# LN2 tiles 2 and 3 turned by VectorE and a DRAM round trip in a DiT block

## The chip, the cores and the metric

The kernel runs on one core of a Trainium2 chip. The metric is device time in microseconds for one execution. Three runs of the kernel before took 243.12, 242.97 and 244.42 us; their median is 243.12 us.

The engines in this document are TensorE (PE; its weight loads are shown apart as PEld), VectorE (DVE), ScalarE (ACT), GpSimd (POOL) and SyncE (SP), which here only issues DMAs. Data lies in SBUF (128 partitions), matmul results in PSUM (8 banks), weights and scratch tensors in DRAM.

## The reference: one diffusion-transformer block

Batch 2, 256 tokens each (512 tokens together), D = 1152, 2 heads of 576, MLP width 4608, everything in bf16:

```python
mod = (_silu(c) @ w_mod).reshape(B, 6, 1, D)
shift_a, scale_a, gate_a, shift_m, scale_m, gate_m = [mod[:, i] for i in range(6)]
h = _layernorm(x) * (1 + scale_a) + shift_a
q, k, v = split(h @ wqkv)                       # per head
a = softmax(q k^T * Dh**-0.5) v @ wo
x = x + gate_a * a
h2 = _layernorm(x) * (1 + scale_m) + shift_m
m = _gelu(h2 @ w_fc1) @ w_fc2
return x + gate_m * m
```

## The kernel before

**Tiling.** Tokens are cut in four tiles of 128 (tile t, batch b = t // 2), D in KT = 9 blocks of 128, the MLP width in JT = 36 blocks of 128. A matmul contracts over the 128 partitions, so before fc1 the normalised tokens must be turned: from `XN2[t]` (token on the partition, 1152 features along it) to the fc1 operand `H2T` (feature on the partition, tokens along it).

**Who orders the work.** The code records every operation with what it reads and writes. TensorE and SyncE keep the order in which the code states them; the other engines' orders come from a list scheduler with modelled costs that always takes the ready operation with the longest modelled way to the end. Waits are then put in from the recorded reads and writes. So a DMA that SyncE issues is never overtaken by one that stands later in the code, and SyncE stops at the first DMA whose wait is not over.

**The stretch around the change.**

- `wo_tile(t)` multiplies by wo in three chunks of 384 columns. Per chunk VectorE multiplies by the gate (L1165), GpSimd adds x (L1166), VectorE takes the LayerNorm statistics (L740). After the third come L741, L743, the `pow` on GpSimd (L744) and L1170 on VectorE, and ScalarE writes the normalised tile `XN2[t]` (L1171).
- `xn2_T(t)` turns a tile: nine 128x128 TensorE transposes (L695) into PSUM, then nine evacuations that apply scale and shift, on VectorE (L1187) and ScalarE (L1190).
- `fc1_tile(f, tok0, ntok)` is one unit of nine matmuls (L692) into one of four rotating PSUM banks; ScalarE reads the bank with a Gelu (L1200) into `GT[f]`. The first F0 = 9 blocks are done in halves: first for tokens 0 to 255, which need only tiles 0 and 1, and later for tokens 256 to 511. Blocks 9 to 35 are done for 512 tokens at once. The transposes of tile 2 stand after the fourth first half, those of tile 3 after the seventh.
- fc1's weights come in nine loads of four blocks each (`wfc1_load(q)`, 1152 KB) into four buffers. Load q = 4, for blocks 16 to 19, goes into the buffer of blocks 0 to 3, and may start once block 3's second half is done; it must have landed before block 16 starts.
- fc2's weights come in four loads of 2592 KB (`ld_wfc2_0` to `_3`). `ld_wfc2_1` and `_2` are issued before the attention output, `ld_wfc2_3` after the fc1 first halves, since its space holds `XN2` too. `ld_wfc2_0` is the last, since its space holds the mlp gate's weights.
- `mlp_gate` computes gate_m on VectorE: 18 operations over 1152 columns (L1092, L1095), a transpose and a reduction (L1099, L1101), and small steps, ordered after the last `h2T` evacuation. The gate goes through DRAM (`dit_scratch`) and is first read when fc2 starts.

SyncE's order from the middle of the kernel on is thus: fc1 loads 0 and 1, the two attention gates, fc1 loads 2 and 3, the mlp gate's weights (`ld_gm`, 2592 KB), `ld_wfc2_1`, `_2`, `_3`, fc1 loads 4 to 8, `ld_wfc2_0`, and the output stores. All its DMAs are recorded at line L673.

Of the kernel before, what the change touches and what calls it, by code (L numbers as in the profile page):

```python
# [73 lines left out]
TRACK_DRAM = set()  # L74
# [417 lines left out]
BF16 = mybir.dt.bfloat16  # L492
F32 = mybir.dt.float32
ALU = mybir.AluOpType
# [3 lines left out]
P = 128  # L498
NTOK = 512
D = 1152  # L500
KT = 9
# [4 lines left out]
SCALE = DH ** -0.5  # L506
CH = 384
NCH = 3
F0 = 9
KC = 5  # L510
KG = 6
NG = 9
# [3 lines left out]
def c_mm(n):  # L516
    return max(n / 2.4 + 2.5, 27.0)


def c_act(n, aps=0):  # L520
    return 190.0 + 0.8 * n + 75.0 * aps
# [18 lines left out]
def c_dve_32(n):  # L540
    return 110.0 + 1.15 * n


def build_kernel(nc, x, c, wqkv, wo, w_mod, w_fc1, w_fc2, out):
# [2 lines left out]
    scratch_t = nc.dram_tensor("dit_scratch", (2, 2, KT * P), BF16)  # L547
    TRACK_DRAM.add("dit_scratch")
    scratch = scratch_t.ap()
    with (  # L550
        nc.sbuf_tensor("arena", [P, ARENA_BYTES // 2], BF16) as arena,
        nc.psum_tensor("psum", [P, 4096], F32) as psum,
# [2 lines left out]
        def sb(off, nbytes, dt=BF16):  # L555
            assert off % 4 == 0 and off + nbytes <= ARENA_BYTES, (off, nbytes)
            v = arena[:, off // 2:(off + nbytes) // 2]
            if dt == F32:
                v = v.bitcast(F32)
            return v  # L560

        def ps32(bank, c0=0, n=512):
            return psum[:, bank * 512 + c0: bank * 512 + c0 + n]

        def ps16(bank, c0=0, n=1024):
            v = psum[:, bank * 512: (bank + 1) * 512].bitcast(BF16)
            return v[:, c0:c0 + n]
# [7 lines left out]
        O_HK = O_HX + 9216  # L575
# [7 lines left out]
        def misc(nbytes):  # L583
            o = mo[0]
            mo[0] += (nbytes + 3) // 4 * 4
            assert mo[0] <= ARENA_BYTES
            return o

        def wmat(o, f):
            return sb(o, KT * f * 2).rearrange("p (k f) -> p k f", k=KT)  # L590
# [12 lines left out]
        WFC2 = sb(O_R, 4 * W1).rearrange("p (k f) -> p k f", k=JT)  # L603
        WFC1 = [wmat(o, 512) for o in (O_A, O_A + 9216, O_C, O_C + 9216)]
# [3 lines left out]
        HK = sb(O_HK, 9216).rearrange("p (k t) -> p k t", k=KT)  # L608
# [1 line left out]
        Q4B = sb(O_Q4B, 1024)  # L610
        X1 = sb(O_QK, 18432, F32).rearrange("p (t d) -> p t d", t=4)
        V = sb(O_HK, 9216).rearrange("p (t d) -> p t d", t=4)
        H2T = HK
        OT = sb(O_HX, 9216).rearrange("p (k t) -> p k t", k=KT)
        PP = [sb(O_P + i * 1024, 1024).rearrange("p (j k) -> p j k", j=2) for i in range(4)]
        PTS = [sb(O_PT + i * 1024, 1024).rearrange("p (j k) -> p j k", j=2) for i in range(4)]
# [2 lines left out]
        XN2 = [sb(O_R + 4 * W1 - (i + 1) * 2304, 2304) for i in range(4)]  # L619
# [25 lines left out]
        SHM = MT[:, 0:288]  # L645
        SC1M = sb(misc(72), 72, F32)
# [22 lines left out]
        wfc2_v = w_fc2.rearrange("(k p) f -> p k f", p=P)  # L669

        def dma(dst, src, nbytes, name, is_out=False, eng="sp", run=4096):
            eff = 1.0 if run >= 4096 else (1.08 if run >= 2304 else (1.15 if run >= 1536 else (1.3 if run >= 1024 else 1.42)))
            return S.op(eng, 500.0 if eng == "sp" else 150.0, lambda e: e.dma_start(dst, src), reads=[src], writes=[dst],  # L673
                        name=name, dma_bytes=nbytes * eff, is_out=is_out)

        def dve(cost, fn, reads, writes, name):
            return S.op("dve", cost, fn, reads=reads, writes=writes, name=name)

        def act(cost, fn, reads, writes, name):
            return S.op("act", cost, fn, reads=reads, writes=writes, name=name)  # L680
# [10 lines left out]
        def mm(o, l, r, st, sp, **kw):  # L691
            S.instr(lambda e: e.matmul(o, lhsT=l, rhs=r, start=st, stop=sp, **kw), reads=[l, r], writes=[o])  # L692

        def tr(o, i_, idn):
            S.instr(lambda e: e.transpose(o, i_, idn), reads=[i_, idn], writes=[o])  # L695
# [59 lines left out]
        for t in range(4):  # L755
# [13 lines left out]
            for part, c0, c1 in ((("a", 0, KC * P), ("b", KC * P, D)) if t == 3 else (("", 0, D),)):  # L769
                xi, xo = X[:, t, c0:c1], XN[:, t, c0:c1]  # L770
                dve(c_dve_fast(c1 - c0), lambda e, xi=xi, xo=xo, m=m, rs=rs: e.tensor_scalar(out=xo, in0=xi, scalar1=m, scalar2=rs,
                                                                                           op0=ALU.subtract, op1=ALU.mult),
# [184 lines left out]
        for kt in range(KT):  # L957
            for b in range(2):
                src, dst = HK[:, kt, b * 256:(b + 1) * 256], HX[:, kt, b * 256:(b + 1) * 256]
                s2 = SHA[:, kt * 32 + b:kt * 32 + b + 1]  # L960
# [159 lines left out]
        def pv_halves():  # L1120
            S.unit("pe", 4 * c_mm(256) + 100.0, "PV_halves")
            for b in range(2):
                for kjt in range(2):
                    for h in range(2):
                        f0 = 512 + 64 * h
                        mm(psum[64 * h:64 * h + 64, 5 * 512 + b * 256:5 * 512 + b * 256 + 256], V[:, 2 * b + kjt, f0:f0 + 64],
                           PTS[b * 2 + h][:, kjt, :], b == 0 and kjt == 0, b == 1 and kjt == 1, skip_group_check=True,
                           tile_position=(0, 64 * h))
            S.order_after(copy_on("dve", OT[:, 4, :], ps32(5), 512, False, "OT_ev_4"), last_mt[0])
# [18 lines left out]
        def acc_bank():  # L1148
            b = acc[acc_rr[0] % len(acc)]
            acc_rr[0] += 1  # L1150
            return b
# [21 lines left out]
        last_h2T = [None]  # L1173

        def xn2_T(t):
            b = t // 2
            xn2 = XN2[t]
            S.unit("pe", KT * c_mm(128), "xn2T_%d" % t)
            hi, lo = ((7, 6), (1, 0))[t % 2]
            slot = [ps16(hi, kt * 128, 128) if kt < 4 else ps16(lo, (kt - 4) * 128, 128) for kt in range(KT)]  # L1180
            for kt in range(KT):
                tr(slot[kt], xn2[:, kt * 128:(kt + 1) * 128], IDENT)
            for kt in range(KT):
                o, dst = slot[kt], H2T[:, kt, t * 128:(t + 1) * 128]
                s1, s2 = SC1M[:, kt * 2 + b:kt * 2 + b + 1], SHM[:, kt * 32 + b:kt * 32 + b + 1]
                if kt < (4 if t < 2 else 6):
                    last_h2T[0] = dve(335, lambda e, o=o, dst=dst, s1=s1, s2=s2: e.tensor_scalar(out=dst, in0=o, scalar1=s1, scalar2=s2, op0=ALU.mult, op1=ALU.add),  # L1187
                        [o, s1, s2], [dst], "h2T_%d_%d" % (t, kt))
                else:
                    act(440, lambda e, o=o, dst=dst, s1=s1, s2=s2: e.activation(out=dst, in_=o, func=ACTF.Identity, scale=s1, bias=s2),  # L1190
                        [o, s1, s2], [dst], "h2T_%d_%d" % (t, kt))

        def fc1_tile(f, tok0, ntok):
            q = f // 4
            S.unit("pe", KT * c_mm(ntok), "fc1_%d_%d" % (f, tok0))
            o = ps32(acc_bank(), 0, ntok)
            for kt in range(KT):
                mm(o, WFC1[q % 4][:, kt, (f % 4) * 128:(f % 4) * 128 + 128], H2T[:, kt, tok0:tok0 + ntok], kt == 0, kt == KT - 1)
            dst = GT[f][:, tok0:tok0 + ntok]
            act(c_act(ntok), lambda e: e.activation(out=dst, in_=o, func=ACTF.Gelu_apprx_tanh), [o], [dst], "gelu_%d_%d" % (f, tok0))  # L1200

# [38 lines left out]
        wfc1_load(2)  # L1240
        wfc1_load(3)
        dma(WGM, wmod_v[:, :, 5 * D:6 * D], D * D * 2, "ld_gm", run=2304)
        for q4 in range(1, 3):
            dma(WFC2[:, 9 * q4:9 * q4 + 9, :], wfc2_v[:, 9 * q4:9 * q4 + 9, :], 9 * P * D * 2, "ld_wfc2_%d" % q4, run=2304)
        pv_halves()
        for b in range(2):
            for h in range(2):
# [2 lines left out]
        wo_tile(1)  # L1250
        wo_tile(2)
        xn2_T(0)
        wo_tile(3, {2: lambda: xn2_T(1)})
        for f in range(0, 4):
            fc1_tile(f, 0, 256)
        xn2_T(2)
        for f in range(4, F0 - 2):
            fc1_tile(f, 0, 256)
        xn2_T(3)
        for f in range(F0 - 2, F0):  # L1260
            fc1_tile(f, 0, 256)
        dma(WFC2[:, 27:36, :], wfc2_v[:, 27:36, :], 9 * P * D * 2, "ld_wfc2_3", run=2304)
        mlp_gate(last_h2T[0])
        k = acc_rr[0] % 4
        acc[:] = [6, 7] + acc[k:] + acc[:k]
        acc_rr[0] = 0
        for f in range(F0):
            fc1_tile(f, 256, 256)
        for f in range(F0, JT):
            if f % 4 == 0 and f // 4 >= 4:  # L1270
# [6 lines left out]
        for t in range(4):  # L1277
            b = t // 2
# [3 lines left out]
            for (c0, c1) in pieces:  # L1282
                w = c1 - c0
                S.unit("pe", JT * c_mm(w), "fc2_%d_%d" % (t, c0))
                o = ps32(acc_bank(), 0, w)
# [22 lines left out]
def bass_standalone__dit_block__diffusion_kernel(  # L1308
    nc: bass.Bass,
    x: bass.AP,  # L1310
    c: bass.AP,
    wqkv: bass.AP,
    wo: bass.AP,
    w_mod: bass.AP,
    w_fc1: bass.AP,
    w_fc2: bass.AP,
    out: bass.AP,
):
    build_kernel(nc, x, c, wqkv, wo, w_mod, w_fc1, w_fc2, out)
# [28 lines left out]
```

## Time and profile before

| What | us |
|---|---|
| Median of the runs (lowest, highest) | 243.12 (242.97, 244.42) |
| Span of the profiled execution | 242.5 |
| TensorE busy, with 1699 matmuls | 237.3 (98%) |
| VectorE busy | 121.5 (50%) |
| ScalarE busy | 67.8 (28%) |
| GpSimd busy | 19.9 (8%) |

The span runs from the first to the last instruction. The profiled execution has no other time of its own than this span; it lies 0.6 us under the median and 0.5 us under the fastest run, which also hold what lies around the span.

In the rows of the profile, L673 is a line of kernel.py; out<-in names what is written and read; nearly every SBUF tensor is a part of one array and so is called `arena`. PE is matmul time, PEld weight loads that run beside it.

### The profile page before, as it was taken

Reading aid. Unit: us, or ns where it says so; the run is one execution under the profiler, and the core shown is the slowest. Engines: PE = TensorE matmul, PEld = TensorE weight load, DVE = VectorE, ACT = ScalarE, POOL = GpSimd, SP = SyncE. Lnnn points to the kernel's source line nnn. Section 1 sums busy time; section 2 is a strip of 40 time slices with the busy share of each in tenths; the row PEclk is TensorE's granted clock in tenths of the full one; section 3 lists DMA queues with packets and bytes.
Section 4 is the critical chain, followed back from the end, with each engine's and each line's share of the span. In section 5 each row is a group of like instructions: output and inputs, shape, how many; then the busy total and the mean of one; then the engine's idle time right before and its main releaser. Section 6 shows DMA issues by size and latency. Waiting matters only on the chain.

```text
span 242.5 us, 3957 instructions
## 1 busy us (share of the span) xinstructions
PE 237.3 (98%) x1699; PEld 145.4 (60%) x1699; DVE 121.5 (50%) x229; ACT 67.8 (28%) x136; POOL 19.9 (8%) x36
## 2 busy tenths in 40 slices
PE   6899999999999999999999999999999999999995
PEld 2688844466666666898544444444666566566564
DVE  2654379988996689669999700000022222111112
ACT  4921440435524206973233322222000000000000
POOL 1300000000002276400000110000000000000000
PEclk9979999999999999999999999999999999999999
DMA  6999999999992999999963499100000000000000
GB/s 221 378 370 392 389 392 390 398 413 402 391 352 79 312 374 391 391 348 398 352 198 83 157 313 374 43 0 3 0 16 19 16 16 16 19 16 16 21 27 20
DMA packets 30363, 51.58 MB, mean 213 GB/s; under 512 B 1547, under 2 KB 15755, under 8 KB 30347
## 3 DMA queue, kind: packets, MB, share of 16 engines
q1 hardware_dynamic: 29888, 50.73, 58.9%
q0 software_dynamic: 288, 0.60, 0.8%
q8 instruction: 13, 0.21, 0.4%
q10 hardware_dynamic: 171, 0.01, 0.0%
q14 instruction: 3, 0.02, 0.0%
HBM read 50.15 MB, written 1.19 MB: 212 GB/s over the span
## 4 chain that ended last, share of the span: by engine, by line
PE 95%; DMA 3%; SPq 1%; DVE 0%; issue 0%
PE psum L692 93%; DMA arena<-in_wqkv_dram 3%; PE psum L695 2%; SPq L673 1%; DVE arena L1290 0%; DVE arena L1291 0%
## 5 line engine op out<-in xcount | busy, mean ns | idle before, releaser
L692 PE MATMUL psum<-arena 128*128 128x384 bf16 (+8 forms) x1610 | 234.0, 314 | 2.4 <-POOL arena L718 1.5
L692 PEld LDWEIGHTS psum<-arena 128*128 128x128 bf16 (+2 forms) x1610 | 139.7, 97 | 92.4 <-issue 3.8
L1290 DVE TENSOR_TENSOR arena<-psum,arena 128x384 f32<-128x384 f32 (+2 forms) x13 | 6.8, 526 | 88.6 <-PE psum L692 88.6
L1200 ACT ACTIVATE arena<-psum 128x512 bf16<-128x512 f32 (+1 forms) x45 | 22.8, 512 | 42.1 <-PE psum L692 42.1
L687 ACT ACTIVATE arena<-psum 128x512 bf16<-128x512 f32 (+6 forms) x34 | 18.2, 560 | 37.9 <-PE psum L692 37.9
L1064 DVE SCALAR_TENSOR_TENSOR arena<-arena 128x1152 f32<-128x1152 bf16 x16 | 21.9, 1408 | 0.0
L1095 DVE SCALAR_TENSOR_TENSOR arena<-arena 128x1152 f32<-128x1152 bf16 x16 | 21.4, 1414 | 0.0
L1166 POOL TENSOR_TENSOR arena<-arena 128x384 f32<-128x384 f32 x12 | 10.9, 912 | 11.7 <-DVE arena L1165 9.5
L740 DVE BATCH_NORM_STATS2 arena<-arena 128x6 f32<-128x384 f32 (+1 forms) x18 | 9.5, 549 | 3.8 <-DMA arena<-in_x_dram 3.8
L673 POOL DMA_DIRECT2D dit_scratch<-arena x4 | 2.4, 609 | 96.6 <-DVE arena L1082 60.3
L689 DVE CAST arena<-psum 128x512 bf16<-128x512 f32 x11 | 7.2, 687 | 5.3 <-PE psum L692 5.3
L1165 DVE TENSOR_TENSOR arena<-psum,arena 128x384 f32<-128x384 f32 x12 | 6.7, 556 | 3.7 <-PE psum L692 3.7
L1171 ACT ACTIVATE arena<-arena 128x1152 bf16<-128x1152 f32 x4 | 5.4, 1344 | 9.8 <-DVE arena L1170 9.8
L695 PE MATMUL psum<-arena 128*128 128x128 bf16 (+1 forms) x89 | 7.4, 225 | 0.4 <-DMA arena<-in_c_dram 0.4
L695 PEld LDWEIGHTS psum<-arena 128*128 128x128 bf16 (+1 forms) x89 | 6.3, 102 | 2.2 <-DMA arena<-in_c_dram 1.1
L1291 DVE TENSOR_TENSOR arena<-arena 128x384 bf16<-128x384 f32 (+2 forms) x13 | 6.9, 527 | 0.5
L1190 ACT ACTIVATE arena<-psum,arena 128x128 bf16<-128x128 bf16 x16 | 6.1, 455 | 3.0 <-PE psum L695 2.2
L1187 DVE TENSOR_SCALAR arena<-psum,arena 128x128 bf16<-128x128 bf16 x20 | 5.5, 336 | 2.9 <-PE psum L695 2.9
L1009 ACT ACTIVATE arena<-psum,arena 128x256 bf16<-128x256 f32 x8 | 3.7, 471 | 0.2 <-DVE arena L1006 0.2
L744 POOL TENSOR_TENSOR arena<-arena 128x1 f32<-128x1 f32 x6 | 3.3, 555 | 4.7 <-DVE arena L743 4.5
L1005 DVE TENSOR_REDUCE arena<-psum 128x2 f32<-128x512 f32 x4 | 2.8, 688 | 0.9 <-PE psum L692 0.7
L962 ACT ACTIVATE arena<-arena 128x256 bf16<-128x256 bf16 x6 | 2.5, 495 | 1.5 <-DVE arena L956 1.5
(60 smaller groups left out, 53.9 us busy)
## 6 DMA issues: line engine op xcount, KB each, us to landing
arena<-in_w_fc_dram SPq DMA_DIRECT2D x9, 1152.0 KB, 8.0
arena<-in_w_fc_dram SPq DMA_DIRECT2D x4, 2592.0 KB, 17.6
arena<-in_wqkv_dram SPq DMA_DIRECT2D x18, 288.0 KB, 9.3
arena<-in_w_mod_dram SPq DMA_DIRECT2D x6, 864.0 KB, 12.3
arena<-in_w_mod_dram SPq DMA_DIRECT2D x3, 1728.0 KB, 20.5
arena<-in_wqkv_dram SPq DMA_DIRECT2D x1, 2592.0 KB, 17.6
arena<-in_wo_dram SPq DMA_DIRECT2D x1, 2592.0 KB, 24.9
arena<-in_w_mod_dram SPq DMA_DIRECT2D x1, 2592.0 KB, 18.5
```

Of the source, the lines that this page charges most:

```text
L687: act(c_act(n), lambda e: e.activation(out=dst, in_=src, func=ACTF.Copy), [src], [dst], name)
L689: return dve(c_dve_psum16(n) if psum16 else c_dve_psum32(n), lambda e: e.tensor_copy(dst, src), [src], [dst], name)
L692: S.instr(lambda e: e.matmul(o, lhsT=l, rhs=r, start=st, stop=sp, **kw), reads=[l, r], writes=[o])
L695: S.instr(lambda e: e.transpose(o, i_, idn), reads=[i_, idn], writes=[o])
L740: dve(550, lambda e, s=s, o=o: e.bn_stats(out=o, in_=s), [s], [o], "bn_%s_%d" % (tag, ci))
L1064: ga_units[(b, kt)] = dve(150 + FG * 1.1, lambda e, o=o, w=w, s1=s1: e.scalar_tensor_tensor(out=o, in0=w, scalar=s1, in1=o, op0=ALU.mult, ...
L1095: u = dve(1300, lambda e, o=o, w=w, s1=s1: e.scalar_tensor_tensor(out=o, in0=w, scalar=s1, in1=o, op0=ALU.mult, op1=ALU.add), [w, s1, o], ...
L1165: dve(550, lambda e, o=o, ga=ga, x1c=x1c: e.tensor_tensor(out=x1c, in0=o, in1=ga, op=ALU.mult), [o, ga], [x1c], "wo_t1_%d_%d" % (t, ci))
L1166: S.op("pool", 930, lambda e, xs=xs, x1c=x1c: e.tensor_tensor(out=x1c, in0=x1c, in1=xs, op=ALU.add), reads=[x1c, xs], writes=[x1c], name=" ...
L1200: act(c_act(ntok), lambda e: e.activation(out=dst, in_=o, func=ACTF.Gelu_apprx_tanh), [o], [dst], "gelu_%d_%d" % (f, tok0))
L1290: dve(c_dve_psum32(w), lambda e, o=o, gm=gm, t1=t1: e.tensor_tensor(out=t1, in0=o, in1=gm, op=ALU.mult), [o, gm], [t1], "fc2_t1_%d_%d" % ( ...
L1291: dve(c_dve_32(w), lambda e, t1=t1, x1c=x1c, ost=ost: e.tensor_tensor(out=ost, in0=t1, in1=x1c, op=ALU.add), [t1, x1c], [ost], "fc2_out_%d ...
```

## The change

Tiles 0 and 1 are turned as before; tiles 2 and 3 no longer by TensorE.

- `xn2_turn(t)`: one VectorE instruction transposes all 32x32 blocks of `XN2[t]` (36 blocks for each group of 32 tokens), reading the features with a step of four, and SyncE stores the result to a DRAM tensor `h_turn[t]`, 288 KB, one run of 2304 bytes per partition.
- `xn2_back(t)`: SyncE loads the tile back, four runs of 576 bytes per partition, which puts each feature on its partition; nine VectorE operations apply scale and shift in place.
- The fc1 operand `H2T` lies in the same bytes in another order: 16 groups of 32 tokens, and in each group the nine feature blocks. A matmul over 256 or 512 tokens now reads runs of 32 tokens (64 bytes), 576 bytes apart, for all four tiles.
- F0 goes from 9 to 14: five more fc1 blocks are done in halves, and no transposes stand among them.
- `ld_wfc2_1` and `_2` are stated after the fc1 first halves, right before `ld_wfc2_3`. In SyncE's order the two stores and two loads of the turn stand where they stood.
- All nine evacuations of tiles 2 and 3 are on VectorE; of tiles 0 and 1, four are on VectorE and five on ScalarE as before.

```diff
-F0 = 9
+F0 = 14
@@ build_kernel
+    p_turn = nc.dram_tensor("p_turn", (4, P, 512), BF16).ap()
+    h_turn = nc.dram_tensor("h_turn", (4, P, D), BF16).ap()
...
-        H2T = HK
+        H2T = sb(O_HK, 9216).rearrange("p (g k i) -> p k g i", g=16, k=KT)
+        H2F = [sb(O_HK + t * 2304, 2304) for t in range(4)]
@@ xn2_T
-                o, dst = slot[kt], H2T[:, kt, t * 128:(t + 1) * 128]
+                o, dst = slot[kt].rearrange("p (g i) -> p g i", i=32), H2T[:, kt, 4 * t:4 * t + 4, :]
...
-                if kt < (4 if t < 2 else 6):
+                if kt < 4:
...
+        def xn2_turn(t):
+            src, flat = XN2[t].rearrange("p (k x c) -> p c k x", k=KT, c=4), H2F[t]
+            dve(c_dve_32(D), lambda e: e.transpose(flat, src), [src], [flat], "h2turn_%d" % t)
+            dma(h_turn[t], flat, P * D * 2, "st_h2_%d" % t)
+
+        def xn2_back(t):
+            b, flat = t // 2, H2F[t]
+            dma(flat.rearrange("p (a y) -> p a y", a=4), h_turn[t].rearrange("(a x) (c y) -> (x c) a y", a=4, c=4), P * D * 2, "ld_h2_%d" % t)
+            for kt in range(KT):
+                dst = H2T[:, kt, 4 * t:4 * t + 4, :]
+                s1, s2 = SC1M[:, kt * 2 + b:kt * 2 + b + 1], SHM[:, kt * 32 + b:kt * 32 + b + 1]
+                last_h2T[0] = dve(200, lambda e, dst=dst, s1=s1, s2=s2: e.tensor_scalar(out=dst, in0=dst, scalar1=s1, scalar2=s2, op0=ALU.mult, op1=ALU.add),
+                    [dst, s1, s2], [dst], "h2T_%d_%d" % (t, kt))
@@ fc1_tile
-                mm(o, WFC1[q % 4][:, kt, (f % 4) * 128:(f % 4) * 128 + 128], H2T[:, kt, tok0:tok0 + ntok], kt == 0, kt == KT - 1)
+                mm(o, WFC1[q % 4][:, kt, (f % 4) * 128:(f % 4) * 128 + 128], H2T[:, kt, tok0 // 32:(tok0 + ntok) // 32, :], kt == 0, kt == KT - 1)
@@ main sequence
         dma(WGM, wmod_v[:, :, 5 * D:6 * D], D * D * 2, "ld_gm", run=2304)
-        for q4 in range(1, 3):
-            dma(WFC2[:, 9 * q4:9 * q4 + 9, :], wfc2_v[:, 9 * q4:9 * q4 + 9, :], 9 * P * D * 2, "ld_wfc2_%d" % q4, run=2304)
         pv_halves()
...
         wo_tile(3, {2: lambda: xn2_T(1)})
-        for f in range(0, 4):
+        xn2_turn(2)
+        xn2_turn(3)
+        xn2_back(2)
+        xn2_back(3)
+        for f in range(0, F0):
             fc1_tile(f, 0, 256)
-        xn2_T(2)
-        for f in range(4, F0 - 2):
-            fc1_tile(f, 0, 256)
-        xn2_T(3)
-        for f in range(F0 - 2, F0):
-            fc1_tile(f, 0, 256)
+        for q4 in range(1, 3):
+            dma(WFC2[:, 9 * q4:9 * q4 + 9, :], wfc2_v[:, 9 * q4:9 * q4 + 9, :], 9 * P * D * 2, "ld_wfc2_%d" % q4, run=2304)
         dma(WFC2[:, 27:36, :], wfc2_v[:, 27:36, :], 9 * P * D * 2, "ld_wfc2_3", run=2304)
         mlp_gate(last_h2T[0])
```

(`p_turn` is not used by any instruction.)

More of the change, by code (lines that the diff above doesn't have):

```diff
@@ L549, in build_kernel @@
     scratch = scratch_t.ap()
+    p_turn = nc.dram_tensor("p_turn", (4, P, 512), BF16).ap()
+    h_turn = nc.dram_tensor("h_turn", (4, P, D), BF16).ap()
+    TRACK_DRAM.add("p_turn")
+    TRACK_DRAM.add("h_turn")
     with (
```

## The prediction

> **What bounds the kernel now.** I read the chain of work that ended last, then the timeline around the change, then when each weight load lands. The chain, in order of time (start, length):
>
> ```profile
> 93.25 0.50 PE psum L695 x9
> 93.75 2.92 PE psum L692 x18
> 96.68 0.50 PE psum L695 x9
> 97.18 5.39 PE psum L692 x45
> 102.57 0.50 PE psum L695 x9
> 103.08 2.95 PE psum L692 x27
> 106.02 0.50 PE psum L695 x9
> 106.53 133.56 PE psum L692 x810
> ```
>
> TensorE never waits here: the end moves by what is added to or taken from its queue. The four groups of nine at L695 are the transposes of LN2, 0.50 us each. 27 matmuls of 256 columns take 2.95, so a half tile of fc1 takes 0.983 and fc1 starts at 102.57 - 4 x 0.983 = 98.64. The Gelus of the full tiles follow each other by 1.942 (timeline):
>
> ```profile
> 130.96 0.37 SPq L673 DMA_DIRECT2D arena<-in_w_fc_dram  x1
> 130.97 0.60 ACT L1200 ACTIVATE arena<-psum 128x512 bf16<-128x512 f32 x1 [1.35 <-PE psum L692]
> 132.91 0.60 ACT L1200 ACTIVATE arena<-psum 128x512 bf16<-128x512 f32 x1 [1.34 <-PE psum L692]
> ```
>
> The DMA at 130.96 is fc1 load 7, which waits for block 15; so block 16 starts at 130.9 (by sum 98.64 + 18 x 0.983 + 1.0 + 7 x 1.942 = 130.9). That is the point I compare.
>
> The second thing is SyncE's queue. Issue to landing, for `ld_gm` with `ld_wfc2_1`, then `ld_wfc2_2`, `ld_wfc2_3`, fc1 loads 4 and 6, each from a stretch that holds its issue:
>
> ```profile
> arena<-in_w_mod_dram SPq DMA_DIRECT2D x1, 2592.0 KB, 18.5
> arena<-in_w_fc_dram SPq DMA_DIRECT2D x1, 2592.0 KB, 21.0
> ...
> arena<-in_w_fc_dram SPq DMA_DIRECT2D x1, 2592.0 KB, 24.3
> ...
> arena<-in_w_fc_dram SPq DMA_DIRECT2D x1, 2592.0 KB, 11.2
> ...
> arena<-in_w_fc_dram SPq DMA_DIRECT2D x1, 1152.0 KB, 8.6
> ...
> arena<-in_w_fc_dram SPq DMA_DIRECT2D x1, 1152.0 KB, 5.5
> ```
>
> With their issues at 79.0, 83.3, 86.6, 106.6, 112.45 and 123.2 the first five land at 97.5, 104.3, 110.9, 117.8 and 121.05: in the order of issue, one 2592 KB load every 6.8 us (390 GB/s), an 1152 KB load 3.2 after the one ahead. Load 6 went out on an empty queue and took 5.5, so 2.3 is fixed. Load 4 lands 9.9 us before block 16 needs it.
>
> **The change, part by part.**
>
> *Transposes of tiles 2 and 3 go:* -2 x 0.50 = -1.0 on the path. *Five more blocks in halves:* 5 x (2 x 0.983 - 1.942) = +0.1.
>
> *Operand in runs of 32 tokens.* The nearest rows are the 72 matmuls of 2x288 for the modulation rows, whose moving operand is read in runs of 32 columns, 256 bytes apart, four at a time in four strips of the array (busy time by stretch; us, PE, PEld, DVE, ACT, POOL, clock, DMA share, GB/s):
>
> ```profile
> 68.90:71.20 2.30, 2.30 (x74) 1.65 (x72) 2.30 (x3) 0.49 (x1) 0.00 (x0) 1.00 1.10 348
> ```
>
> 18 groups of 288 columns in 2.2 to 2.3 us are 122 to 128 ns a group, the pace of contiguous operands (384 columns in 162 ns: 122 for 288). So I take 0. If 64-byte runs at a pitch of 576 cost a tenth, that is 0.1 a half tile and 0.19 a full one.
>
> *Statistics.* The scheduler now puts tile 2's aggregation behind two of tile 3's statistics. In the trace these run from 99.2 by 0.54 each; so tile 2's variance is ready at 101.1 rather than 99.3, `pow` (0.55) ends at 101.75, and ScalarE writes XN2 2 from 102.0 (101.0 before) and XN2 3 from 103.3 to 104.6 (1.34 each). The Gelu of block 2 stands behind both, and block 6 needs its bank at 104.4: it starts near 105.0, so +0.6. Block 16's weightless start is then 130.9 - 1.0 + 0.1 + 0.6 = 130.6.
>
> *The turn.* Transposes of 1152 f32 took 1356 ns, of 2304 2578 (1.06 a column); 96 bf16 took 267 against 278 for 96 f32, so bf16 is no faster there. Two by 1.36: 103.4 to 104.75 and to 106.0. Stores: an output store of 96 KB lands in 1.6, one of 20 KB in 1.4, so 288 KB in about 2.1: 106.9 and 108.2. Loads of 288 KB: 2.3 + 0.8 by load 6; a scratch load of that size took 4.3, the slowest 6.6; with runs of only 576 bytes I take 3.4. SyncE issues load 2 at 106.95 and load 3, which waits for store 3, at 108.3; they land at 110.4 and 111.7. Eighteen evacuations at 0.15 to 0.2 (twelve of 256 columns at L965 are 2.4 us busy) end at 113.2. TensorE comes to the second halves at 98.64 + 14 x 0.983 + 0.6 = 113.0 and to the ninth feature block at 113.9. It doesn't wait, with under a microsecond to spare; the five extra half tiles are that cover.
>
> *What is queued behind the turn.* All three fc2 loads now stand behind load 3 of the turn on SyncE, and fc1 load 4 behind them. So:
> - `ld_wfc2_1` is issued at 108.3 + 0.4 = 108.7 (83.3 before) and lands at 108.7 + 2.3 + 6.8 = 117.8, `_2` at 124.6, `_3` at 131.4;
> - fc1 load 4 (its buffer is free at 113.0 + 3.9 = 116.9) lands 3.2 later, at 134.6.
>
> Block 16 is ready at 130.6, so TensorE waits 4.0 us there. This wait swallows what came before it: the gained 0.9 and the 0.6. Block 16 starts at 134.6 instead of 130.9: **+3.7**. Nothing later is late: load 5 lands at 137.8 and is needed at 142.4; load 8 waits for block 19 as before; `mlp_gate` starts 5 us later (113.2 for 108.1) and its gate lands near 155, `ld_wfc2_0` near 157, fc2 starts near 173.5 (130.9 + 20 x 1.942 + 3.7).
>
> Sum: 242.5 + 3.7 = 246.2 for the profiled span; the median lies 0.6 above the span, so **246.8**.
>
> Bounds of the landing. Low: turn 3 costs 0.6, stores 1.6, and 9.14 MB move at 415 GB/s (the best stretches): issue at 107.3, landing at 131.6, +0.7. High: stores take 4.3 like the scratch rows, the loads run at 360 GB/s as from 84 to 88 us: issue at 110.8, landing at 138.5, +7.6. I stand near the middle, as four landings in a row went by 6.6 to 6.9.
>
> The Trainium skill, "DMA: Bandwidth & Descriptors", Specifications, gives a fabric ceiling of 435 GB/s and an HBM limit of about 358 per core; by the first load 4 would land at an estimated 132.0 (+1.1), by the second at 136.5 (+5.6). The landings here, 390, lie between.
>
> **Rivals.**
>
> *The clock falls in the wait.* The trace shows it once, early, after a stretch of short matmuls with gaps (clock is the third number from the right):
>
> ```profile
> 10.00:12.00 2.00, 1.79 (x25) 1.43 (x26) 1.69 (x8) 1.97 (x3) 0.46 (x1) 0.79 1.04 408
> 12.00:14.00 2.00, 2.00 (x11) 1.44 (x10) 1.68 (x4) 0.79 (x2) 0.00 (x0) 0.50 1.05 387
> 14.00:16.00 2.00, 2.00 (x22) 1.88 (x21) 0.96 (x4) 0.00 (x0) 0.55 (x1) 0.86 1.13 356
> ```
>
> What is missing from 1.00 adds up to 2 x (0.21 + 0.50 + 0.14) = 1.7 us, some 3.4 us at half clock. If 4.0 us of idleness set this off, +1.7: 248.5. Against it: no wait of such length occurs in the trace. The Trainium skill, "TensorE: Matmul & The Clock Gate", Part 1, says that one free-running window of about 3.4 us without work halves the clock; by that rule a wait of 4.0 holds a whole window about one time in six, and partly idle windows decide the rest.
>
> *Not slower: the loads come in time.* If load 4 landed by 130.6, the time would be 242.8 (-1.0 + 0.1 + 0.6), or 242.2 without the Gelu's delay. That needs 9.14 MB in 19.6 us, 466 GB/s, which no stretch shows, or `ld_wfc2_1` issued at 104.7, before the second transpose can end. In part it can be: within 1% of before means landing by 133.3, 1.3 us earlier than I say, by a cheaper turn or 415 GB/s; say 132.5, which gives 244.7.
>
> *The turn comes back late.* With 4.3 for a store and 6.6 for a load, tile 3 is back at 117.1, TensorE waits 4 us at the second halves and again for load 4 (136.8): +5.9, 249.0. For it: the cover is under 1 us; against: those rows shared the queue or were broadcasts.
>
> *Reads of 64 bytes are costly.* A tenth on fc1: the first 28 half tiles' loss lies in the wait, the 22 full tiles add 22 x 0.19 = 4.2: 251.0. The 2x288 row speaks against it.
>
> **Chances.** Forecast (246.8, own range 245.4 to 248.2) 0.48; clock falls 0.24; loads partly in time (244.7) 0.14, wholly 0.03; turn late 0.07; costly 64-byte reads 0.04. The range 244.0 to 249.8 leaves out the costly reads, the loads in time and the outer ends. A measurement here tells about 1% from no change (2.4 us): slower by more 0.82, within 0.16, faster by more 0.02.
>
> **What would show it.** In the profile after: one idle stretch of TensorE of some 4 us at fc1 block 16, released by a DMA of fc1 weights; no idle time, or little, at the first second half; SyncE's `h_turn` DMAs between 104 and 109 us and a DMA share near nothing from 97 to 108, then full to 134; VectorE transposes near 1.36; a clock of 1.00 after the wait. I am wrong if the fc2 loads go out before 106, if fc1's matmuls are slower by the row, or if load 4 lands out of order.

## The result, and the profile after

The changed kernel took 252.51 us in the median of four runs (252.16 to 255.0), the kernel before 243.12 (242.97 to 244.42): a ratio of 1.0409, 95% interval 1.0375 to 1.0443. It is slower by 9.4 us, in the direction of the forecast, but above its range (244.0 to 249.8).

The chain of work that ended last in the changed kernel, from the last tile of wo on (start, length, what; "issue" is time in which the engine waited for nothing that the profile shows):

```profile
97.57 1.48 PE psum L697 x9
...
102.12 1.36 ACT arena L1176
...
103.50 1.39 DVE arena L1200
...
104.91 3.01 DMA h_turn<-arena
107.91 0.02 issue
107.93 2.99 DMA arena<-h_turn
110.92 0.03 issue
110.95 2.33 DVE arena L1209 x10
113.28 0.05 issue
113.33 5.04 PE psum L697 x37
118.37 19.34 DMA arena<-in_w_fc_dram
137.71 0.14 issue
137.84 110.76 PE psum L697 x648
```

Before, this was TensorE from end to end. Now it runs through the whole turn (statistics, ScalarE, VectorE, store, load, evacuations), and then 19.34 us lie on one DMA: fc1 load 4, issued at 118.37 and landed at 137.71. Block 16 starts at 137.84; before, at 130.93.

TensorE's wait (us in total, times, longest), and then the busy time by stretch around it (us, PE, PEld, DVE, ACT, POOL, clock, DMA share, GB/s):

```profile
PE psum L697 <- DMA arena<-in_w_fc_dram: 5.8, 1, 5.8
```

```profile
130.00:132.00 2.00, 2.00 (x10) 0.72 (x8) 2.00 (x2) 0.60 (x1) 0.00 (x0) 1.00 1.05 387
132.00:134.00 2.00, 0.05 (x1) 0.00 (x0) 2.00 (x3) 0.60 (x1) 0.00 (x0) 1.00 1.08 359
134.00:136.00 2.00, 0.00 (x0) 0.00 (x0) 2.00 (x2) 0.00 (x0) 0.00 (x0) 1.00 1.10 348
136.00:138.00 2.00, 0.16 (x1) 0.14 (x2) 1.97 (x3) 0.00 (x0) 0.00 (x0) 0.84 1.10 349
138.00:140.00 2.00, 2.00 (x6) 0.68 (x5) 2.00 (x1) 0.00 (x0) 0.00 (x0) 0.50 1.10 347
140.00:142.00 2.00, 2.00 (x9) 0.83 (x8) 1.97 (x2) 0.58 (x1) 0.00 (x0) 0.80 1.11 349
```

TensorE idles from 132.05 to 137.84 while the DMA engines are full, and then works at half clock: by the clock column 2 x (0.16 + 0.50 + 0.20) = 1.7 us of clock are missing, a part of them still in the wait. From block 16 to the last matmul it took 110.76 us, before 240.08 - 130.93 = 109.15: +1.6.

The first fc2 load after the turn was issued at 109.03:

```profile
arena<-in_w_fc_dram SPq DMA_DIRECT2D x1, 2592.0 KB, 11.8
```

It landed at 120.8. The two behind it followed at 127.5 and 134.3, 6.7 and 6.8 apart, and load 4 at 137.7, 3.4 later.

### The profile page after: what moved, and what is told of

The parts are those of the page before. It is cut to its first block, busy times and chain, and to the rows that moved or that the text cites. A ratio compares the mean times of both kernels' runs of the same rounds, so it can differ in the third digit from the quotient of the medians.

```text
span 251.1 us, 4021 instructions
## 1 busy us (share of the span) xinstructions
PE 239.3 (95%) x1726; PEld 148.4 (59%) x1726; DVE 124.9 (50%) x237; ACT 66.6 (27%) x135; POOL 20.2 (8%) x36
## 4 chain that ended last, share of the span: by engine, by line
PE 81%; DMA 13%; DVE 3%; SPq 1%; ACT 1%; issue 0%; POOL 0%
PE psum L697 80%; DMA arena<-in_w_fc_dram 8%; DMA arena<-in_wqkv_dram 3%; DMA h_turn<-arena 1%; DMA arena<-h_turn 1%; PE psum L700 1%; SPq L678 1%; DVE arena L1209 1%; DVE arena L745 1%; DVE arena L1200 1%; ACT arena L1176 1%; POOL arena L749 0%; DVE arena L1170 0%; DVE arena L1307 0%; DVE arena L1308 0%
## 5 line engine op out<-in xcount | busy, mean ns | idle before, releaser
L697 PE MATMUL psum<-arena 128*128 128x384 bf16 (+8 forms) x1655 | 236.8, 311 | 8.8 <-DMA arena<-in_w_fc_dram 5.8
L697 PEld LDWEIGHTS psum<-arena 128*128 128x128 bf16 (+2 forms) x1655 | 144.1, 97 | 97.9 <-issue 11.9
L1219 ACT ACTIVATE arena<-psum 128x256 bf16<-128x256 f32 (+1 forms) x50 | 23.4, 476 | 51.6 <-PE psum L697 51.6
L1209 DVE TENSOR_SCALAR arena<-arena 128x128 bf16<-128x128 bf16 x18 | 4.1, 308 | 4.8 <-DMA arena<-h_turn 4.8
L700 PE MATMUL psum<-arena 128*128 128x128 bf16 (+1 forms) x71 | 5.7, 218 | 0.5 <-DMA arena<-in_c_dram 0.5
L700 PEld LDWEIGHTS psum<-arena 128*128 128x128 bf16 (+1 forms) x71 | 4.8, 98 | 2.1 <-DMA arena<-in_c_dram 1.2
L1195 ACT ACTIVATE arena<-psum,arena 128x128 bf16<-128x128 bf16 x10 | 3.8, 454 | 2.2 <-PE psum L700 2.2
L1200 DVE STREAM_TRANSPOSE arena<-arena 128x1152 bf16<-128x1152 bf16 x2 | 2.6, 1356 | 0.9 <-ACT arena L1176 0.9
## 6 DMA issues: line engine op xcount, KB each, us to landing
arena<-in_w_mod_dram SPq DMA_DIRECT2D x6, 864.0 KB, 12.3
```

## The experiments

**The order of SyncE's loads, and nothing else.** (`wfc2_load(q4)` is one fc2 load as before, written as a function.) My theory was that block 16 waits because load 4 stands behind three fc2 loads; its rival, that the turn itself, its DMAs or the 64-byte operand runs cost the time.

```diff
-        for q4 in range(1, 3):
-            dma(WFC2[...], ..., "ld_wfc2_%d" % q4, run=2304)
-        dma(WFC2[:, 27:36, :], ..., "ld_wfc2_3", run=2304)
+        wfc2_load(1)
         mlp_gate(last_h2T[0])
...
             if f % 4 == 0 and f // 4 >= 4:
                 wfc1_load(f // 4)
+                if f in (24, 28):
+                    wfc2_load(2 if f == 24 else 3)
```

> The changed kernel with two fc2 loads stated later: after the turn SyncE issues ld_wfc2_1, then fc1 loads 4, 5, 6, ld_wfc2_2, load 7, ld_wfc2_3, load 8, ld_wfc2_0. Theory (queue order): load 4 stands behind one 2592 KB load instead of three and lands near 124, so the wait of 5.8 us at block 16 goes and with it the half clock after it (1.6): 252.5 - 7.4 = 245.1 us, clock 1.00 around 135 to 142. Rival (the turn itself, its DMAs or the 64-byte operand runs cost the time): stays above 250.

Measured 243.81 us against 243.17 of before in the same set, 1.0039 (1.0011 to 1.0067). The chain's last long piece:

```profile
109.46 2.33 DVE arena L1209 x10
111.80 0.05 issue
111.84 127.88 PE psum L697 x792
```

No wait at block 16, the clock at 1.00 there. Two loads moved down in one queue take 8.7 us off the changed kernel (7.6 against its second set, below), with the turn, its DMAs and the 64-byte runs all in place: the theory holds, and the rival is out as the cause of the 9.4. I had expected 245.1. The missing 1.3 is near the price of one more spell of half clock (1.1 to 1.6, below): three of the changed kernel's four runs have a mean clock of 0.986, which is two such spells, and three of the four runs here have 1.00.

**The two fc2 loads ahead of the turn, as before the change.**

```diff
         dma(WGM, ..., "ld_gm", run=2304)
+        for q4 in range(1, 3):
+            dma(WFC2[...], ..., "ld_wfc2_%d" % q4, run=2304)
...
         for f in range(0, F0):
             fc1_tile(f, 0, 256)
-        for q4 in range(1, 3):
-            dma(WFC2[...], ..., "ld_wfc2_%d" % q4, run=2304)
```

> The changed kernel with ld_wfc2_1 and _2 stated where they stood before the change, ahead of the turn. Theory (one queue in order): the stores, issued at 105, land only behind 5.3 MB of fc2 weights, near 111, the loads near 115, so TensorE waits some 3 to 4 us at the first second half and not at block 16: 245.1 + 3.5 = 248.6 us. Rival (small transfers pass large ones): the turn takes as long as in the changed kernel, no wait anywhere, 245.1.

Measured 249.56 us, 1.0258 (1.0231 to 1.0284), by the theory's mechanism and a microsecond above its number. That the number is so near is partly luck: it was added to an expected 245.1 that came out as 243.81, and over that the delay cost 5.8 us where 3.5 was expected.

```profile
104.96 7.01 DMA h_turn<-arena
111.97 0.02 issue
111.99 2.94 DMA arena<-h_turn
114.93 0.03 issue
114.95 2.33 DVE arena L1209 x10
117.28 0.05 issue
117.33 128.69 PE psum L697 x792
```

The stores now take 7.0 us instead of 3.0, TensorE waits 4.2 us for the evacuations, until 117.3, and from there on for nothing. The clock fell to half after this wait too. So with the turn on SyncE, loads ahead of it make the turn late, and three loads behind it make load 4 late.

**The turn on GpSimd's own DMA queue**, with the fc2 loads early.

```diff
-            dma(h_turn[t], flat, P * D * 2, "st_h2_%d" % t)
+            dma(h_turn[t], flat, P * D * 2, "st_h2_%d" % t, eng="pool")
...
-            dma(flat..., h_turn[t]..., P * D * 2, "ld_h2_%d" % t)
+            dma(flat..., h_turn[t]..., P * D * 2, "ld_h2_%d" % t, eng="pool")
```

> The kernel of x2 (ld_wfc2_1 and _2 stated early) with the four turn DMAs issued by GpSimd, which has a DMA queue of its own, instead of SyncE. Theory (order within SyncE's queue, not the load on the DMA engines, made x2's stores wait): the stores land in 3 to 4 us rather than 7, tile 3 is back near 113, TensorE waits about 2 us at the second halves instead of 4, nothing at block 16: 246.5. Rival (the DMA engines are full, whatever the queue): as x2, 249.6.

Measured 252.53 us, 1.0392 (1.0365 to 1.0419): worse than on SyncE's queue. The theory fell, and the rival is too mild:

```profile
103.90 5.76 DMA h_turn<-arena
109.66 0.28 issue
109.94 6.60 DMA arena<-h_turn
116.54 0.03 issue
116.56 2.33 DVE arena L1209 x10
118.90 0.05 issue
118.94 129.64 PE psum L697 x792
```

The stores gain 1.2 us over x2, but the loads take 6.6 instead of 2.9. SyncE no longer stops at the turn, so `ld_wfc2_3` goes out ahead of the loads of the turn, and from 96 to 116 the DMA engines move 368 to 407 GB/s without a break. So a queue of its own did not carry the turn past the weight loads; in x2 the turn's own wait on SyncE kept the third load away from its loads. That full DMA engines alone make a load on GpSimd's queue this slow is not shown: in x2 its two loads of 288 KB for the mlp gate, issued at 154.20 and 154.79 while 387 to 396 GB/s were moved, landed in 3.7 and 3.8 us. Whether GpSimd's queue or the runs of 576 bytes have a part in the 6.6 was not tested.

**The operand in groups of 32 tokens alone,** on the kernel before.

```diff
-        H2T = HK
+        H2T = sb(O_HK, 9216).rearrange("p (g k i) -> p k g i", g=16, k=KT)
...
-                o, dst = slot[kt], H2T[:, kt, t * 128:(t + 1) * 128]
+                o, dst = slot[kt].rearrange("p (g i) -> p g i", i=32), H2T[:, kt, 4 * t:4 * t + 4, :]
...
-                mm(o, ..., H2T[:, kt, tok0:tok0 + ntok], kt == 0, kt == KT - 1)
+                mm(o, ..., H2T[:, kt, tok0 // 32:(tok0 + ntok) // 32, :], kt == 0, kt == KT - 1)
```

> The kernel before with the fc1 operand in groups of 32 tokens alone (written by the evacuations, read by all fc1 matmuls in runs of 64 bytes). Theory (reads of 64 bytes cost nothing): 243.1, fc1's Gelus 1.94 apart. Rival (they cost a tenth): 250.

Measured 243.35, 1.0006 (0.9992 to 1.002). Two successive Gelus of full tiles:

```profile
122.20 0.60 ACT L1200 ACTIVATE arena<-psum 128x512 bf16<-128x512 f32 x1 [1.35 <-PE psum L692]
124.14 0.60 ACT L1200 ACTIVATE arena<-psum 128x512 bf16<-128x512 f32 x1 [1.34 <-PE psum L692]
```

1.94 apart: reads in runs of 64 bytes cost nothing here. Nor do the writes; the evacuations average 336 and 455 ns in both kernels.

**The two tensors declared, not used.**

```diff
     scratch = scratch_t.ap()
+    p_turn = nc.dram_tensor("p_turn", (4, P, 512), BF16).ap()
+    h_turn = nc.dram_tensor("h_turn", (4, P, D), BF16).ap()
```

> The kernel before with the two DRAM tensors declared and not used. The changed kernel's runs are 1.7 us longer than their spans, the median of before only 0.6 longer than the span of its profile. If declaring the tensors costs time outside the span: 244.2. If not: 243.1, and the difference has another source.

Measured 243.16 against 243.17, 0.9999 (0.9985 to 1.0013). They cost nothing, and the runs of before on this chip show where my question came from: 243.17 with a span of 241.4 and a mean clock of 1.00. A run is 1.7 to 1.8 us longer than its span with both kernels; the profile that I predicted from, with its span of 242.5, was of an execution 1.1 us longer than usual, the one with the half clock between 11 and 15 us. Of 30 runs of before beside the experiments 28 had a clock of 1.00, and two had 0.993 and took 244.5 and 244.7.

**The changed kernel again**, as the base for the next ones (no edit).

> The changed kernel unaltered, on the chip of the three below, as their base: 252.5 us, a wait near 5.8 us at block 16, half clock after it.

Measured 251.37 against 243.09, 1.0339 (1.0308 to 1.0371). Its profile has the wait (from 130.06 to 135.95) and the half clock after it, and no low clock early. It lies 1.1 us under the first set, and what sets the two apart is open: all four runs of the first set and three of the four here have a mean clock of 0.986 or lower. The profiled one here has 0.993, one spell; where the second spell of the others lay, early or in a longer one at block 16 as in x7 (below), can't be seen, since one execution of a set is profiled.

**The wait filled with matmuls** that nobody reads.

```diff
         for f in range(F0, JT):
+            if f == 16:
+                for i in range(24):
+                    S.unit("pe", 215.0, "fill_%d" % i)
+                    mm(ps32(0), IDENT, GT[0], True, True)
```

> The changed kernel with 24 matmuls of 512 columns on the identity (5.2 us) put ahead of block 16, into a PSUM bank that nobody reads. Theory (idleness halves the clock): TensorE idles under 1 us there, the clock stays 1.00 and 1.6 us come back: 250.9. Rival (the low clock comes from something else, the full DMA queues for one): clock 0.8, 0.5, 0.8 again and no gain, 252.5.

Measured 250.65, 0.7 under x0 in the same set. The stretch around block 16:

```profile
132.00:134.00 2.00, 2.00 (x11) 0.90 (x10) 2.00 (x2) 0.00 (x0) 0.00 (x0) 1.00 1.10 349
134.00:136.00 2.00, 1.41 (x7) 0.50 (x6) 1.97 (x3) 0.00 (x0) 0.00 (x0) 1.00 1.10 348
136.00:138.00 2.00, 2.00 (x11) 0.91 (x10) 2.00 (x1) 0.05 (x1) 0.00 (x0) 1.00 1.11 349
```

The clock stays at 1.00 with the DMA engines as full as before, so idleness lowers it and not the transfers. From block 16 to the last matmul it took 109.31 us (x0: 110.63): 1.3 saved of the 1.6 expected. The trace shows it; the medians alone would not, since 0.7 is within the spread (x6's four runs, all at a clock of 0.999 or 1.00, lie up to 1.5 us apart, and why is open).

**The loads of the turn as whole rows**, so that fc1 works on an operand that is not turned.

```diff
-            dma(flat.rearrange("p (a y) -> p a y", a=4), h_turn[t].rearrange("(a x) (c y) -> (x c) a y", a=4, c=4), ...)
+            dma(flat, h_turn[t], ...)
```

> The changed kernel with the two turn loads read back as they were stored, one run of 2304 bytes per partition in place of four of 576; fc1 so works on an operand that is not turned. Theory (1024 packets of 576 bytes hold the queues ahead of the fc2 loads): ld_wfc2_1 lands some 2 us earlier, all behind it too, and the wait at block 16 shrinks to about 3.8: 250.5. Rival (a 2592 KB load on an empty queue needs 11 to 12 us whatever stands ahead): 252.2.

Measured 252.34 (x0: 251.37), and the first fc2 load, issued at 107.36, landed no sooner:

```profile
arena<-in_w_fc_dram SPq DMA_DIRECT2D x1, 2592.0 KB, 12.3
```

The theory that the 576-byte packets hold up the fc2 loads fell.

**The turn's DMAs cut to an eighth**, most of the operand left as VectorE wrote it.

```diff
-            dma(h_turn[t], flat, P * D * 2, "st_h2_%d" % t)
+            dma(h_turn[t][0:16], flat[0:16], 16 * D * 2, "st_h2_%d" % t)
...
-            dma(flat.rearrange(...), h_turn[t].rearrange(...), P * D * 2, "ld_h2_%d" % t)
+            dma(flat[0:16], h_turn[t][0:16], 16 * D * 2, "ld_h2_%d" % t)
```

> The changed kernel with the turn's DMAs cut to 16 partitions (36 KB each instead of 288); the rest of the fc1 operand is the block-transposed tile as VectorE left it, so the turn is incomplete. What counts is issue to landing of ld_wfc2_1 (11.8 in the changed kernel, 12.3 with whole rows read back, 9.1 in my sum). Theory A (the 0.6 MB of the two turn loads ahead of it take its place): 9.1 to 9.8, and with an issue some 1.2 us earlier the wait at block 16 is near 2.5: 248.5. Theory B (a first 2592 KB load takes this long by itself): above 11, wait near 4.6: 250.

Measured 250.48 us, in the set of x5. The first fc2 load, issued at 107.11, and the DMA rate from then on:

```profile
arena<-in_w_fc_dram SPq DMA_DIRECT2D x1, 2592.0 KB, 10.1
```

```profile
106.00:108.00 2.00, 2.00 (x21) 1.79 (x19) 0.51 (x3) 0.77 (x2) 0.00 (x0) 1.00 0.23 51
108.00:110.00 2.00, 2.00 (x21) 1.78 (x20) 2.00 (x11) 0.77 (x2) 0.00 (x0) 1.00 0.86 185
110.00:112.00 2.00, 2.00 (x21) 1.80 (x19) 2.00 (x9) 0.77 (x2) 0.00 (x0) 1.00 1.04 411
```

10.1 lies between the theories. The time and the wait do not tell them apart: the wait was 5.5 us, above both, since TensorE too came to block 16 earlier (at 128.89; in x0 at 130.06). By bytes the turn's loads are worth about 1.5 us of the 11.6 to 11.8 of the changed kernel (an estimate: 0.59 MB at 390 GB/s), and 10.1 - 6.8 = 3.3 remains for the start of the load, where my sum had 2.3.

The other traces don't bear out that the turn's bytes are the cause. With the whole turn ahead the same load took 11.2 in x1, 12.3 in x2 and x7, but 9.4 in x9 (below), where the turn's two loads were issued 1.8 us apart instead of 0.7. What differs is how fast the rate comes up: in stretches of two microseconds from the issue on, the DMA engines moved 259, 288, 347 and 399 GB/s in the changed kernel, and 161, 396, 411 and 396 in x9. Why it comes up so late in the changed kernel is open. What is issued behind the load is not the main reason: in x1 nothing was for the next 9 us, and it took 11.2.

**A version that beats both:** x1's order, sixteen blocks in halves, and tile 3's first statistics held until tile 2's variance is ready (`veps_unit[0]` is the operation that ends tile 2's variance; the lines of x1 are left out).

```diff
-F0 = 14
+F0 = 16
...
-                dve(550, lambda e, s=s, o=o: e.bn_stats(out=o, in_=s), [s], [o], "bn_%s_%d" % (tag, ci))
+                u = dve(550, lambda e, s=s, o=o: e.bn_stats(out=o, in_=s), [s], [o], "bn_%s_%d" % (tag, ci))
+                if tag == "ln2_3" and ci == 0:
+                    S.order_after(u, veps_unit[0])
```

> Loads in the order of x1, 16 blocks in halves instead of 14, and tile 3's first statistics held until tile 2's variance is ready, so that a Gelu stands between the two XN2 again. Theory (the 0.64 us by which x1 is over before are the Gelu's hold, 0.45, and the late evacuations at the second halves, 1.1, less the 0.9 gained): both go, 2 x 0.02 is paid: 242.4, TensorE without idle time. Rival (the rest of x1 is due to TensorE reading or to the DMA traffic): 243.8.

Measured 242.55 us against 243.09 (12 and 17 runs), 0.9974 (0.9957 to 0.9991), 0.15 from the expected time. TensorE is without a wait again from the last transposes to the end:

```profile
95.50 0.50 PE psum L700 x9
96.01 142.06 PE psum L697 x945
```

So the gain in the change is the microsecond of transposes that the prediction counted, and half a microsecond of it, 0.3%, can be had once nothing waits. In the spans more of it is seen, 240.5 against 241.4 in the medians; but these runs lie 1.7 to 2.7 us above their spans instead of 1.7 to 1.8, and why is open. The two edits on top of x1 were not tried apart.

## Why the prediction was wrong

Between the two profiles the span grew by 251.1 - 242.5 = 8.6. It comes apart as: +0.4, since this whole execution began later (the first weights of the K projection let TensorE go at 11.31 instead of 10.81, and 18.18 stands for 17.79 further on), which has nothing to do with the change; +3.7 as in the sum; +2.7 for a later landing; +0.1 from landing to matmul; +1.6 from block 16 to the end, nearly all of it the clock (x6, at full clock, took 109.31 there, 1.45 less). The rest of 0.1 is rounding.

**Right, and shown by x1:** the place and the mechanism. TensorE gained 0.9 us and lost it at block 16, to a load that SyncE's order had put behind three others. The turn's steps stood nearly where the prediction put them: transposes at 1356 ns; loads 3.0 and 3.3 us for 3.4; stores 3.0 and 2.4 for 2.1; `ld_wfc2_1` issued at 109.03, which is 108.6 without the late start, for 108.7. The intervals of 6.8 and 3.2 us held as well (6.7, 6.8, 3.4).

**Wrong: the term "108.7 + 2.3 + 6.8 = 117.8" for the first fc2 load.** It measured 11.8 from issue to landing instead of 9.1, and everything behind it came 2.7 later. The 2.3 was taken from a load that found the queue empty; but the turn's own two loads had just gone into the same queue, and the rate reached 390 GB/s only some six microseconds after the issue (x10 above). The prediction named those loads as what `ld_wfc2_1` is issued behind, and counted their issue, not their bytes. Six traces with the turn's full loads ahead of it on SyncE's queue show 11.2 to 12.3 us for this load. How much of the 2.7 is the turn's bytes (about 1.5 by estimate) and why the rate comes up late is open, since in x9 the turn has the same bytes and the load took 9.4.

**Wrong: the forecast left the clock out of the likeliest case.** "The clock falls in the wait" had a chance of 0.24 and a price of 1.7; it fell in each of the six profiled kernels where TensorE waited four microseconds or more, and cost 1.6 here. I weighed it for a wait of 4.0 us; it fell after 4.2 in x2 as well. x6 shows that idleness is the cause. The Trainium skill, "TensorE: Matmul & The Clock Gate", Part 1, gives a free-running window of about 3.4 us as the unit; by that rule a wait of 5.8 holds, by estimate, a whole window seven times in ten. The traces agree on the unit: the half clock lasted 3.4 us here, in x0, x2 and x10, 6.8 in x7 and 10.2 in x5. They do not agree that a whole window must be idle, and the measurement decides: in x5 TensorE had been idle for 2.6 us when the clock fell, and 0.79 of the 3.41 us before the fall were matmul.

**Wrong, without effect on the time:** that TensorE "doesn't wait" at the second halves. The evacuations take 228 ns each where I took 150 to 200 (eighteen in 4.10 us), and the matmuls of the first second half followed them one by one, so that it ended 1.3 us late (x1: 1.2). The Gelu's hold cost 0.27: in the changed kernel the matmuls before and after it start 0.38 apart instead of 0.11, in x1 as well. The 0.6 foreseen had block 6 at 104.4 where its own terms give 98.64 + 6 x 0.983 = 104.5, and the 0.45 that I expected x9 to win back was too much. The wait at block 16 swallowed both delays. x1, where that wait is gone, pays them, 0.27 + 1.2, and has the 0.9 gained: 0.6, and it stays 0.64 above before. x9 shows neither.

**The base.** I took the median to lie 0.6 above a span; every run of before and of the changed kernel with both numbers has 1.7 to 1.8. The profile of before was of a run 1.1 us longer than usual, with the half clock early. The changed kernel's profile had the same spell, so the difference of the spans (8.6) is free of it, while the first set's median difference is 9.4 and the second's 8.3.

**A reading.** "4.3, the slowest 6.6" for scratch loads are medians of two loads each (3.6 and 4.9 on SyncE's queue, 6.7 and 6.5 on GpSimd's); the high bound of the landing and the rival of the late turn rest on them, not the sum. That VectorE's transpose is no faster in bf16 was read off two small ones of different shape; the turn's own, 1356 ns as for f32, bear it out.

By its own terms the prediction with 11.8 for 9.1 and with the clock would have given 242.5 + 3.7 + 2.7 + 1.6, a span of 250.5 and a time of 251.1 to 252.2, depending on the base.

## What to carry to other kernels

In this kernel, a DMA that waits in the middle of SyncE's queue moves everything stated behind it, so the price of a new round trip is read at the next load that somebody needs, not at the round trip. Order that queue by when each load is needed; here two loads moved were worth 7.6 to 8.7 us. A wait of TensorE of four microseconds or more is to be counted with the clock's fall behind it: it fell in all six such waits here, of 4.2 to 7.4 us.

## What the runs showed of the hardware

The clock doesn't fall at once: the granted clock went to 0.50 after TensorE had fallen idle 5.3 us earlier in the changed kernel and in x10, 5.2 in x0, 4.3 in x2 (0.1 after it had started again), 3.5 in x7 and 2.6 in x5. In x7 and x5 it fell 2.9 and 4.8 us before the wait ended, so a part of the low spell cost nothing.

The spell of half clock in the first 16 us of this program, where short matmuls alternate with gaps, comes and goes between executions of the same kernel: the profiles of before, the changed kernel and x2 have it, those of x3, x0 and x1 don't. With it the profile of before is 1.1 us longer; the runs of before at a mean clock of 0.993 are 1.4 to 1.6 longer, though no trace shows where their spell lay. No single gap before it was longer than 0.6 us; in the 3.41 us ahead of the fall TensorE was busy for 2.66 in the profile of before. A profile should be checked for it before its span is taken as a base.
